# Second operand of the decay scans in two PSUM banks, scans cut to at most three chunk runs, decay copies on ScalarE

## The chip, the core and the metric

The kernel runs on one core of a Trainium2 chip. The metric is the device time of one execution in microseconds (us), smaller is better. The core's engines work side by side, each through its own queue in order: TensorE (PE in the profile; PEld is its weight load), VectorE (DVE), ScalarE (ACT), GpSimd (POOL), and SP, whose queue here issues all transfers (DMA). An engine waits for another through semaphores. SBUF is the working memory of 128 partitions; PSUM is a second, smaller one of eight banks of 512 float32 columns per partition, into which TensorE writes its products.

## What is computed

A recurrent (gated linear) attention over 4 batches, 8 heads, 768 steps and 48 dimensions, then a soft mixture of experts, then a gated MLP with RMS normalisation, on 3,072 tokens of width 384:

```python
for t in range(S):                                   # attention, per batch and head
    state = alpha[t][:, None] * state + outer(k[t], v[t])
    y[t] = q[t] @ state
logits = x @ phi                                     # soft mixture of 8 experts, 32 slots
slot_out = relu(softmax(logits, 0).T @ x @ w1) @ w2  # per expert
x = softmax(logits, 1) @ slot_out
xn = x / rms(x) * rms_g                              # gated MLP
out = (silu(xn @ w_gate) * (xn @ w_val)) @ w_out
```

## The kernel before

**Attention in chunks.** The 768 steps of each batch are cut into chunks of 128, 24 chunks in all. Two heads lie together on the partitions (rows 0 to 47 and 64 to 111), so a chunk has four head pairs. Inside a chunk the decay is taken out of the recurrence: R is the running product of alpha from the chunk's first step, q is multiplied by R, and k by an inverse decay iR, so that the chunk's scores are plain products of k and q, masked to the lower triangle. The state between chunks is multiplied by the chunk's whole decay.

**Preparation of a group.** Chunks are prepared in units of three (the first two units have one and two), each unit in two groups of two head pairs; there are 17 groups. A group is a row of "chunk runs" of 129 columns, one leading column and 128 steps: six runs, 774 columns, in the large groups, four runs, 516 columns, in the first three. For each group:

- `prep_R` (L465, VectorE): one scan over all runs. At each column it multiplies the running value by alpha and takes the maximum with the second operand `d1`, which is 1 at the start of each run (it restarts the product there) and a tiny floor elsewhere.
- `prep_i` (L471, L472, VectorE): reciprocals of the runs' last R are written into `d2`, then one scan backwards over all runs with `d2` as second operand makes iR.
- `prep_c` (L481, L482, GpSimd): two small copies of the runs' whole decay, one for the state (`gm`), one for a check (`chk`).
- `prep_m` (L487, VectorE): k times iR and q times R.

`d1` and `d2` lie in SBUF, in a block of 776 columns each.

**A chunk.** TensorE makes the scores of the head pairs (L523) into two PSUM banks; ScalarE copies these two (L530); GpSimd masks them (L534); TensorE makes the outputs (L559, L566) and the state's update (L546, L550), which VectorE multiplies by the decay (L572, one operand in PSUM, one in SBUF). The scores of even chunks go to the pair of banks `sc`, those of odd chunks to the pair `tr` (`sc_of`, L507).

**Weights beside it.** The gate weights, 64 bits wide in memory, are turned to float32 meanwhile in `wide_ops`: load (L385, SP), L388 and L389 (ScalarE), L392 (VectorE), L399 and L400 (GpSimd), L403 (VectorE); three landing blocks and two sets of temporaries are all they have. The experts' weights (L738 for w1, L740 for w2, 64 loads of 384 KB) go to blocks of SBUF as these come free. The working memory has 58 such blocks.

**What sets the order.** `Plan` is a list scheduler: each step has an engine, a cost, a priority and the ring places it takes (`new`) or uses (`use`). Before any instruction is made, it walks through the steps in time by these costs and fixes the order of each engine's queue, SP's included. The semaphores follow from the data.

After attention, `join`, `experts` (hidden products L751, results L772) and `gated` (72 rounds of L1029, L1031, L1033, L1036 and their products) come in turn.

## Time and profile before

| | |
|---|---|
| three runs | 445.19, 443.86, 442.87 us; median 443.86 |
| profiled execution | 441.4 us; span from first to last instruction 439.7 us |
| busy: TensorE, VectorE, ScalarE, GpSimd | 387.5, 304.6, 222.3, 198.2 us |
| chain that ended last | PE 53%, DVE 17%, POOL 14%, issue 6%, DMA 5%, ACT 2% |
| mean granted clock of TensorE | 0.952 |
| transfers | 65.4 MB, mean 149 GB/s |

The busy times are sums over a span whose parts have different limits, so they don't say what bounds one part; the tables by stretch do. A group is all instructions of one line, engine and form, with their count, busy time, mean duration and the idle time of the engine before them. An instruction that waits for something after it has started shows as a long instruction, not as idle time. The chain is followed back from the last instruction, at each step to what released it.

### The profile page before, as it was taken

How to read it: one execution, taken by the hardware profiler on the slowest of the kernel's cores; microseconds unless marked ns; L12 is line 12 of the kernel's file. 1: busy time of each engine (PE TensorE's matmuls, PEld its weight loads, DVE VectorE, ACT ScalarE, POOL GpSimd, SP SyncE). 2: the span in 40 equal slices, each digit the busy share in tenths (PEclk: the TensorE clock that was granted, in tenths of full speed). 3: DMA queues.
4: the chain of work that ended last, by engine and by line, in shares of the span. 5: the costliest groups of instructions: out<-in, count | busy, mean ns of one | idle time of the engine just before them, and what ended most of it. 6: DMA issues, size and time to landing. Idle time of an engine off the chain costs nothing.

```text
span 439.7 us, 9033 instructions
## 1 busy us (share of the span) xinstructions
PE 387.5 (88%) x3435; PEld 320.4 (73%) x3435; DVE 304.6 (69%) x494; ACT 222.3 (51%) x465; POOL 198.2 (45%) x281
## 2 busy tenths in 40 slices
PE   6688957589488699999987999999999999999994
PEld 6566735466366577764445798999999999999993
DVE  8999798999998978261169987655554655664550
ACT  1424463267345456361277756645546555546441
POOL 3488788869988788141131683130220210310000
PEclk8889996969889869999999999999999999999999
DMA  7879997887575768989932300200101001002002
GB/s 239 270 245 306 288 271 264 256 258 210 149 183 162 233 218 283 337 290 345 382 114 87 108 2 0 73 0 15 59 2 37 35 1 70 3 1 73 1 2 79
DMA packets 28758, 65.43 MB, mean 149 GB/s; under 512 B 4096, under 2 KB 10368, under 8 KB 28704
## 3 DMA queue, kind: packets, MB, share of 16 engines
q1 hardware_dynamic: 28704, 64.75, 45.7%
q8 instruction: 29, 0.48, 0.5%
q14 instruction: 25, 0.20, 0.2%
HBM read 60.01 MB, written 4.72 MB: 147 GB/s over the span
## 4 chain that ended last, share of the span: by engine, by line
PE 53%; DVE 17%; POOL 14%; issue 6%; DMA 5%; ACT 2%; SPq 0%; DVEq 0%; POOLq 0%; ACTq 0%
POOL b L400 4%; POOL b L534 3%; POOL b L399 3%; PE pssc L996 3%; PE pstr L996 3%; DVE b L487 3%; DVE b L465 3%; PE psy L1003 3%; PE pskn L1003 3%; PE psmisc L1005 3%; PE psU L1005 3%; PE pskn L1005 3%; PE psy L1005 3%; PE psU L1003 3%; PE psmisc L1004 3%
## 5 line engine op out<-in xcount | busy, mean ns | idle before, releaser
L1036 DVE TENSOR_TENSOR b<-b,b 128x512 fp32r<-128x512 f32 (+1 forms) x73 | 51.9, 712 | 52.5 <-PE psmisc L1005 24.6
L1033 ACT CAST b<-b 128x512 fp32r<-128x512 f32 (+1 forms) x73 | 44.8, 615 | 46.3 <-DVE b L1031 44.5
L1031 DVE TENSOR_TENSOR b<-b,pssc 128x512 f32<-128x512 f32 (+1 forms) x73 | 49.2, 676 | 15.7 <-ACT b L1029 13.6
L1029 ACT ACTIVATE b<-pstr 128x512 f32<-128x512 f32 (+1 forms) x73 | 43.1, 594 | 31.5 <-PE pstr L996 24.1
L534 POOL TENSOR_SCALAR_AFFINE_SELECT b<-b 128x512 f32<-128x512 f32 x48 | 50.1, 1061 | 13.2 <-ACT b L530 13.1
L559 PE MATMUL psy<-b,b 128*48 128x128 f32 x384 | 32.8, 303 | 11.8 <-POOL b L534 10.3
L388 ACT ACTIVATE b<-b 128x384 f32<-128x384 f32 x36 | 20.2, 562 | 44.9 <-DVE b L403 34.0
L400 POOL TENSOR_TENSOR b<-b,b 128x384 int32<-128x384 int32 x26 | 40.1, 1543 | 2.0
L933 POOL TENSOR_TENSOR sq<-st 128x4 f32<-128x4 f32 x5 | 1.5, 301 | 87.4 <-DVE st L918 87.4
L559 PEld LDWEIGHTS psy<-b,b 128*48 128x48 f32 x384 | 23.9, 135 | 20.7 <-POOL b L534 14.0
L403 DVE SCALAR_TENSOR_TENSOR b<-b,b 128x384 int32<-128x384 int32 x36 | 27.9, 777 | 10.0 <-POOL b L400 10.0
L399 POOL TENSOR_TENSOR b<-b,e 128x384 int32<-128x384 int32 x26 | 29.6, 1139 | 10.8 <-DVE b L392 9.0
L487 DVE TENSOR_TENSOR b<-b,b 128x768 f32<-128x768 f32 (+1 forms) x33 | 34.2, 1066 | 0.3
L465 DVE TENSOR_TENSOR_SCAN b<-b,b 128x774 f32<-128x774 f32 (+1 forms) x17 | 33.9, 1992 | 0.1
L472 DVE TENSOR_TENSOR_SCAN b<-b,b 128x774 f32<-128x774 f32 (+1 forms) x17 | 32.0, 1881 | 0.9
L996 PE MATMUL pssc<-b,b 128*128 128x512 f32 (+1 forms) x73 | 28.7, 394 | 0.4 <-DVE b L1031 0.4
L996 PE MATMUL pstr<-b,b 128*128 128x512 f32 (+1 forms) x73 | 28.6, 392 | 0.1
L1114 ACT COPY y<-psy 128x512 f32<-128x512 f32 x24 | 14.1, 586 | 28.4 <-PE psy L566 23.1
L566 PE MATMUL psy<-b,b 48*48 48x128 f32 x320 | 24.1, 295 | 1.8 <-DVE b L572 1.8
L1005 PE MATMUL pskn<-b,b 128*128 128x384 f32 x72 | 24.5, 341 | 1.1 <-DVE b L1036 1.0
L1003 PE MATMUL pskn<-b,b 128*128 128x384 f32 x72 | 24.8, 345 | 0.0
L1003 PE MATMUL psU<-b,b 128*128 128x384 f32 x72 | 24.5, 340 | 0.0
(241 smaller groups left out, 986.4 us busy)
## 6 DMA issues: line engine op xcount, KB each, us to landing
b<-in_moe_w_dram SPq DMA_DIRECT2D x64, 384.0 KB, 6.1
b<-in_v_rows_dram SPq DMA_DIRECT2D x24, 192.0 KB, 4.4
b<-in_moe_w_gate_dram SPq DMA_DIRECT2D x12, 384.0 KB, 3.8
b<-in_moe_w_out_dram SPq DMA_DIRECT2D x12, 384.0 KB, 5.1
b<-in_moe_w_val_dram SPq DMA_DIRECT2D x12, 384.0 KB, 3.1
out_dram<-b SPq DMA_DIRECT2D x24, 192.0 KB, 1.9
b<-in_alpha_rows_dram SPq DMA_DIRECT2D x24, 145.3 KB, 4.2
b<-in_k_rows_dram SPq DMA_DIRECT2D x18, 144.0 KB, 4.7
```

What stands on the lines that cost most here:

```text
L400: G.tensor_tensor(ui, ui, r(), ALU.add)
L465: V.tensor_tensor_scan(plan("R", (u, g))[:, 0:w], plan("al", (u, g))[:, 0:w], d1[:, 0:w], 1.0, ALU.mult, ALU.max)
L487: eng.tensor_tensor(t, t, r, ALU.mult)
L534: G.affine_select(s, s, pattern=[[0, NP], [1, C]], compare_op=ALU.is_ge, fill=0.0, base=0, channel_multiplier=-1)
L559: T.matmul(y[64 * a:64 * a + D, p, :], vv[:, h], heads(plan("scS", (n, a)))[:, p, :], start=p == 0, stop=first and p == NP - 1)
L996: T.matmul(plan(r, ("gv", j, f))[:, s], G4(f // 3, a)[:, f % 3 * P:(f % 3 + 1) * P], plan("Q", ("c4", j))[:, s].bitcast(F32R), start=True, ...
L1003: T.matmul(po, h, wo_of(f)[:, 0, :], start=(f == 0), stop=False)
L1005: T.matmul(po, l, wo_of(f)[:, 0, :], start=False, stop=(f == NF - 1))
L1029: plan.op(part("sg"), "ACT", 51 + 427 / np, pg, lambda g=g, SG=SG, s=s: A.activation(SG()[:, s], plan(*g)[:, s], AF.Silu), [part("gv"), *p ...
L1031: plan.op(part("mu"), "DVE", 69 + 533 / np, pg, lambda val=val, SG=SG, s=s: V.tensor_tensor(SG()[:, s], SG()[:, s], plan(*val)[:, s], ALU. ...
L1033: plan.op(part("hh"), "ACT", 93 + 427 / np, pg, lambda SG=SG, HH=HH, s=s: A.copy(HH()[:, s], SG()[:, s]), [part("mu"), *pre("hh")], new=ne ...
L1036: lambda SG=SG, HH=HH, HL=HL, s=s: V.tensor_tensor(HL()[:, s], SG()[:, s], HH()[:, s], ALU.subtract), [part("hh"), *pre("hl")], new=new(hl),
```

## The change

The second operands `d1` and `d2` move from two blocks of SBUF to the two PSUM banks `tr`, as wide as three chunk runs and one column. Scans and reciprocals therefore go over at most three runs at a time: two pieces for each group (of three runs, 387 columns, or of two, 258). The `tr` banks are taken from the start by a step without an engine (`pb`) and come free when the last inverse scan is planned (`pe`); until then, and also after, the scores of all chunks use the `sc` banks alone. The two small copies of a group go from GpSimd to ScalarE, with a cost of 400 ns in place of 450. The two blocks of SBUF are free for weights from the start. Nothing else is edited; since the planner sees other places and costs, the order of the steps in attention changes too. Lines of the changed kernel are 3 to 12 higher than before.

```diff
--- before.py
+++ after.py
@@ -281,10 +281,10 @@
 
     BL, CW = 768, 384
     LAY = [("wT", BL, 2 * KD * FF // BL), ("Tk", BL, PLACES["k"]), ("Tq", BL, PLACES["q"]), ("al", BCOLS, PLACES["a"]), ("R", BCOLS, 3), ("iR", BCOLS, 2), ("scS", NP * C, 4), ("St", NP * D, 2),
-           ("knS", DM, 1), ("vt", DM, 5), ("cv", 2 * CW, 3), ("cu", CW, 2), ("cr", CW, 2), ("d1", BCOLS, 1), ("d2", BCOLS, 1),
+           ("knS", DM, 1), ("vt", DM, 5), ("cv", 2 * CW, 3), ("cu", CW, 2), ("cr", CW, 2),
            ("fa", 2 * NP * NCH, 1), ("mask", C, 1), ("chk", NP * NCH, 1), ("gm", NP * J, 3)]
 
-    GROUPS = [set(s.split()) for s in ("wT", "Tk", "Tq", "al", "R", "iR", "scS St fa mask chk gm", "knS vt", "cv", "cu cr", "d1", "d2")]
+    GROUPS = [set(s.split()) for s in ("wT", "Tk", "Tq", "al", "R", "iR", "scS St fa mask chk gm", "knS vt", "cv", "cu cr")]
     room, inside, where = [], [], {}
     for nm, size, n in LAY:
         for i in range(n):
@@ -348,11 +348,14 @@
         return t.rearrange("k (n p) -> k n p", n=NP)
 
     St = [heads(t) for t in rings["St"]]
-    d1, d2, mask, chk = (rings[x][0] for x in ("d1", "d2", "mask", "chk"))
+    mask, chk = (rings[x][0] for x in ("mask", "chk"))
+
+    RUNS = 3
+    d1, d2 = (banks["tr"][i][:, 0:RUNS * (C + 1) + 1] for i in range(2))
     chk = chk.rearrange("p (a b) -> p a b", a=NP)
     phiP = rings["phi"][0].rearrange("p (n s) -> p n s", n=NP)
     V.memset(d1, FLOOR)
-    V.memset(d1[:, 0:6 * C1].rearrange("p (m x) -> p m x", x=C1)[:, :, 0:1], 1.0)
+    V.memset(d1[:, 0:RUNS * C1].rearrange("p (m x) -> p m x", x=C1)[:, :, 0:1], 1.0)
     V.memset(d2, FLOOR)
     V.memset(banks["y"][0], 0.0)
     V.memset(banks["U"][0][:, 0:NP * D], 0.0)
@@ -459,17 +462,25 @@
 
         return t[:, at:at + units[u][2][g][1] * units[u][1] * C1].rearrange("k (m x) -> k m x", x=C1)
 
+    def scans(u, g):
+        m = units[u][1] * units[u][2][g][1]
+        n = -(-m // RUNS)
+        return [(m * i // n * C1, m * (i + 1) // n * C1) for i in range(n)]
+
     def prep_R(u, g):
 
-        w = PIECES["a"][u, g][0] - 1
-        V.tensor_tensor_scan(plan("R", (u, g))[:, 0:w], plan("al", (u, g))[:, 0:w], d1[:, 0:w], 1.0, ALU.mult, ALU.max)
+        al, R = plan("al", (u, g)), plan("R", (u, g))
+        for x, y in scans(u, g):
+            V.tensor_tensor_scan(R[:, x:y], al[:, x:y], d1[:, 0:y - x], 1.0, ALU.mult, ALU.max)
 
     def prep_i(u, g):
 
-        w = slice(1, PIECES["a"][u, g][0])
-        al = plan("al", (u, g))
-        V.reciprocal(runs(d2, u, g, 1)[:, :, C:C1], runs(plan("R", (u, g)), u, g)[:, :, C:C1])
-        V.tensor_tensor_scan(plan("iR", (u, g))[:, w][:, ::-1], al[:, w][:, ::-1], d2[:, w][:, ::-1], 1.0, ALU.mult, ALU.max)
+        al, R, iR = plan("al", (u, g)), plan("R", (u, g)), plan("iR", (u, g))
+        for x, y in scans(u, g):
+            run = lambda t: t.rearrange("k (m x) -> k m x", x=C1)[:, :, C:C1]
+            w, d = slice(x + 1, y + 1), d2[:, 1:y - x + 1]
+            V.reciprocal(run(d), run(R[:, x:y]))
+            V.tensor_tensor_scan(iR[:, w][:, ::-1], al[:, w][:, ::-1], d[:, ::-1], 1.0, ALU.mult, ALU.max)
 
     def prep_c(u, g):
 
@@ -478,8 +489,8 @@
         pc = lambda t: t.rearrange("k (p c) x -> k p c x", c=j)
         if g == 0:
             gmU[u] = plan("gm", u).rearrange("k (p c) -> k p c", c=J)
-        G.tensor_copy(gmU[u][:, p0:p0 + n, 0:j], pc(runs(plan("R", (u, g)), u, g))[:, :, :, C])
-        G.tensor_copy(chk[:, p0:p0 + n, c0:c0 + j], pc(runs(plan("iR", (u, g)), u, g))[:, :, :, 1])
+        A.copy(gmU[u][:, p0:p0 + n, 0:j], pc(runs(plan("R", (u, g)), u, g))[:, :, :, C])
+        A.copy(chk[:, p0:p0 + n, c0:c0 + j], pc(runs(plan("iR", (u, g)), u, g))[:, :, :, 1])
 
     def prep_m(nm, u, g, eng):
         t = plan(RING[nm], (u, g))[:, 0:PIECES[nm][u, g][0]].rearrange("k (m x) -> k m x", x=C)
@@ -504,7 +515,7 @@
         return [(r, (u, g)) for g in range(len(units[u][2]))]
 
     def sc_of(n):
-        return [("tr" if n % 2 else "sc", (n, a)) for a in range(2)]
+        return [("sc", (n, a)) for a in range(2)]
 
     def turn_k(n, p):
         T.transpose(heads(plan("kn", n))[:, p, :], kq("Tk", n, p), ident)
@@ -1062,6 +1073,7 @@
         plan.op(("wu", i), "PE", 436, 1e6, lambda i=i: warm(plan("misc", ("wu", i)), 4), new=[("misc", ("wu", i))])
 
 
+    plan.op("pb", "X", 0, 0, lambda: None, new=[("tr", "d1"), ("tr", "d2")])
     plan.op("phi", "SP", 900, 0, load_phi, [("v", 1)])
     last = {}
     for u, (c0, j, groups) in enumerate(units):
@@ -1073,7 +1085,7 @@
                 last[nm] = [("l", nm, x)]
             plan.op(("R", x), "DVE", 40 + 2.3 * w, t, lambda x=x: prep_R(*x), [("l", "a", x)], new=[("R", x)], use=[("al", x)])
             plan.op(("I", x), "DVE", 220 + 2.3 * w, t, lambda x=x: prep_i(*x), [("R", x)], new=[("iR", x)], use=[("R", x), ("al", x)])
-            plan.op(("ck", x), "Pool", 450, t + CK, lambda x=x: prep_c(*x), [("I", x), *([("ck", (u, 0))] if g else [])], new=[] if g else [("gm", u)], use=[("R", x), ("iR", x)])
+            plan.op(("ck", x), "ACT", 400, t + CK, lambda x=x: prep_c(*x), [("I", x), *([("ck", (u, 0))] if g else [])], new=[] if g else [("gm", u)], use=[("R", x), ("iR", x)])
             for nm in "kq":
                 e, en, cost = (G, "Pool", 2.6 * w) if (nm, u) in BY_POOL else (V, "DVE", 60 + 1.05 * w)
                 plan.op((nm, x), en, cost, t, lambda nm=nm, x=x, e=e: prep_m(nm, *x, e), [("l", nm, x), ("R" if nm == "q" else "I", x)],
@@ -1115,7 +1127,7 @@
         plan.op(("x", n), "PE", 436, n + XD, lambda n=n: xnat(n), [("ye", n)], new=[x_bank(n)], use=[("yT", n)])
         plan.op(("xe", n), "ACT", 480, n + XD, lambda n=n: move_x(n), [("x", n)], new=[("xN", n)], use=[x_bank(n)])
 
-    plan.op("pe", "X", 0, 0, lambda: None, [x for x in plan.ops if x[0] == "I"], new=[("d1", 0), ("d2", 0)])
+    plan.op("pe", "X", 0, 0, lambda: None, [x for x in plan.ops if x[0] == "I"], use=[("tr", "d1"), ("tr", "d2")])
     plan.op("se", "X", 0, 0, lambda: None, [("o", NCH - 1)], new=[("St", 0), ("St", 1), ("mask", 0)])
     for i in range(NCH // 4):
         group(plan, i, phiP, NP, 4 * i + 3 + GD)
```

VectorE's queue, the preparation of one group in mid attention. Before; `b_142` is `d1`, `b_143` is `d2`, L392 and L403 belong to the gate weights:

```order
L465 SCALAR_TENSOR_TENSOR b_125<-b_124,b_142 128x774
L392 TENSOR_SCALAR b_140<-b_140 128x384
L403 SCALAR_TENSOR_TENSOR b_103<-b_137,b_140 128x384
L471 RECIPROCAL b_143<-b_125 128x6
L472 SCALAR_TENSOR_TENSOR b_129<-b_124,b_143 128x774
L403 SCALAR_TENSOR_TENSOR b_103<-b_138,b_140 128x384
L487 TENSOR_TENSOR b_117<-b_117,b_129 128x768
L487 TENSOR_TENSOR b_122<-b_122,b_125 128x768
```

After; `pstr_63` is `d1`, `pstr_64` is `d2`:

```order
L474 SCALAR_TENSOR_TENSOR b_125<-b_124,pstr_63 128x387 x2
L406 SCALAR_TENSOR_TENSOR b_103<-b_137,b_140 128x384
L395 TENSOR_SCALAR b_140<-b_140 128x384
L482 RECIPROCAL pstr_64<-b_125 128x3
L483 SCALAR_TENSOR_TENSOR b_129<-b_124,pstr_64 128x387
L482 RECIPROCAL pstr_64<-b_125 128x3
L483 SCALAR_TENSOR_TENSOR b_129<-b_124,pstr_64 128x387
L498 TENSOR_TENSOR b_117<-b_117,b_129 128x768
```

Each scan and the reciprocal have become two (`x2` is the pair in one row), with 387 columns in place of 774, and a reciprocal stands ahead of each backward piece.

ScalarE's queue, a little earlier in the program, around the copies of one chunk's scores. Before; the L388 and L389 are the gate weights' first steps:

```order
L582 COPY x<-psmisc_70 128x384
L388 ACTIVATE b_140<-b_138 128x384
L389 ACTIVATE b_141<-b_138 128x384
L530 COPY b_132<-pstr_63 128x512
L530 COPY b_133<-pstr_64 128x512
L388 ACTIVATE b_140<-b_139 128x384
L389 ACTIVATE b_141<-b_139 128x384
L1114 COPY y_146<-psy_69 128x512
L388 ACTIVATE b_140<-b_137 128x384
```

After (L391 and L392 are the gate weights, L541 the score copies, L492 and L493 the decay copies):

```order
L593 COPY x<-psmisc_70 128x384
L391 ACTIVATE b_140<-b_139 128x384
L392 ACTIVATE b_141<-b_139 128x384
L541 COPY b_130<-pssc_65 128x512
L541 COPY b_131<-pssc_66 128x512
L492 COPY b_130<-b_127 128x6
L493 COPY b_133<-b_128 128x2x3
L391 ACTIVATE b_140<-b_137 128x384
L392 ACTIVATE b_141<-b_137 128x384
L528 COPY b_134<-pskn_67 128x384
```

The scores come from `pssc` alone, and the two decay copies of a group stand in this queue, here behind the score copies and ahead of the next gate weight.

SP's queue at about a third of the preparation. Before (L738 are expert weights):

```order
L385 DMA b_138<-in_moe_w_gate_dram 128x768
L453 DMA b_118<-in_q_rows_dram 48x768 x2
L738 DMA b_879<-in_moe_w_dram 128x768
L456 DMA b_135<-in_v_rows_dram 128x384 x2
L453 DMA b_124<-in_alpha_rows_dram 48x775 x2
L385 DMA b_139<-in_moe_w_gate_dram 128x768
L453 DMA b_114<-in_k_rows_dram 48x768 x2
L453 DMA b_119<-in_q_rows_dram 48x768 x2
```

After (L749 are expert weights):

```order
L388 DMA b_138<-in_moe_w_gate_dram 128x768
L456 DMA b_118<-in_q_rows_dram 48x768 x2
L749 DMA b_949<-in_moe_w_dram 128x768
L459 DMA b_135<-in_v_rows_dram 128x384
L749 DMA b_959<-in_moe_w_dram 128x768
L749 DMA b_962<-in_moe_w_dram 128x768
L388 DMA b_139<-in_moe_w_gate_dram 128x768
L459 DMA b_135<-in_v_rows_dram 128x384
L388 DMA b_137<-in_moe_w_gate_dram 128x768
```

Three expert loads stand where one stood.

## Rows read from the trace of the kernel before

**Rows 1.** Stretches: busy us of each engine, granted clock, DMA share, GB/s.

```profile
0.00:168.00 168.00, 129.24 (x1581) 98.05 (x1581) 152.95 (x202) 78.53 (x174) 133.20 (x136) 0.88 0.78 238
168.00:194.00 26.00, 25.18 (x367) 19.26 (x367) 13.79 (x44) 13.42 (x34) 12.92 (x22) 1.00 0.94 324
194.00:222.00 28.00, 26.46 (x344) 12.23 (x344) 5.30 (x17) 6.69 (x16) 4.62 (x15) 1.00 0.92 340
```

**Rows 2.** Chain of waits, 20 to 168 us: shares by line.

```profile
by line: issue 13.4%; POOL b L400 11.4%; POOL b L534 10.3%; POOL b L399 10.1%; DVE b L487 5.7%; DVE b L403 4.7%; DMA b<-in_moe_w_gate_dram 4.7%; DVE b L472 4.1%; DVE b L465 4.1%; PE psy L559 3.1%; DVE b L392 3.0%; POOL b L482 2.5%; PE pssc 
```

**Rows 3.** Groups on VectorE, 0 to 168 us: count, busy us, mean ns, idle.

```profile
L465 DVE TENSOR_TENSOR_SCAN b<-b,b 128x774 f32<-128x774 f32 x14 | 30.2, 2157 | 0.0
L487 DVE TENSOR_TENSOR b<-b,b 128x768 f32<-128x768 f32 x28 | 30.0, 1100 | 0.2
L472 DVE TENSOR_TENSOR_SCAN b<-b,b 128x774 f32<-128x774 f32 x14 | 28.3, 2020 | 0.8
L403 DVE SCALAR_TENSOR_TENSOR b<-b,b 128x384 int32<-128x384 int32 x24 | 19.8, 824 | 9.0 <-POOL b L400 9.0
...
L472 DVE TENSOR_TENSOR_SCAN b<-b,b 128x516 f32<-128x516 f32 x3 | 3.7, 1232 | 0.2
...
L471 DVE RECIPROCAL b<-b 128x6 f32<-128x6 f32 x14 | 2.6, 184 | 0.1
```

**Rows 4.** Groups on GpSimd, 0 to 168 us.

```profile
L534 POOL TENSOR_SCALAR_AFFINE_SELECT b<-b 128x512 f32<-128x512 f32 x42 | 46.1, 1114 | 8.2 <-ACT b L530 8.1
L400 POOL TENSOR_TENSOR b<-b,b 128x384 int32<-128x384 int32 x24 | 37.9, 1578 | 1.9
L399 POOL TENSOR_TENSOR b<-b,e 128x384 int32<-128x384 int32 x24 | 27.9, 1162 | 10.5 <-DVE b L392 8.7 <-ACT b L388 1.7
L482 POOL COPY b<-b 128x6 f32<-128x6 f32 (+1 forms) x17 | 11.9, 702 | 7.4 <-DVE b L472 3.5 <-PE pstr L523 1.9 <-PE psmisc L629 1.9
L481 POOL COPY b<-b 128x6 f32<-128x6 f32 (+1 forms) x17 | 10.2, 598 | 1.7 <-DVE b L465 1.6
```

**Rows 5.** Order of time, 71.3 to 73 us: start us, us, instruction.

```profile
71.45 0.35 DVE L572 TENSOR_TENSOR b<-psU,b 128x192 f32<-128x192 f32 x1
71.61 0.83 POOL L399 TENSOR_TENSOR b<-b,e 128x384 int32<-128x384 int32 x1 [0.95 <-DVE b L392]
...
71.71 2.35 DVE L465 TENSOR_TENSOR_SCAN b<-b,b 128x774 f32<-128x774 f32 x1
...
72.52 2.33 POOL L400 TENSOR_TENSOR b<-b,b 128x384 int32<-128x384 int32 x1
```

**Rows 6.** Order of time on VectorE around 51 us.

```profile
51.01 1.77 DVE L472 TENSOR_TENSOR_SCAN b<-b,b 128x774 f32<-128x774 f32 x1
```

**Rows 7.** Single lines: shortest, median and longest instruction in ns.

```profile
L572 DVE TENSOR_TENSOR b<-psU,b x20: 325/344/358, 23.5 to 183.5; 128x192 f32<-128x192 f32 x20
...
L399 POOL TENSOR_TENSOR b<-b,e x26: 824/856/2291, 36.5 to 170.6; 128x384 int32<-128x384 int32 x26
...
L400 POOL TENSOR_TENSOR b<-b,b x26: 992/1198/2349, 37.4 to 171.6; 128x384 int32<-128x384 int32 x26
...
L534 POOL TENSOR_SCALAR_AFFINE_SELECT b<-b x48: 630/760/2147, 11.7 to 181.2; 128x512 f32<-128x512 f32 x48
```

**Rows 8.** Single lines: second operand in PSUM (L1031), in SBUF (L487).

```profile
L1031 DVE TENSOR_TENSOR b<-b,pssc x73: 415/686/691, 237.1 to 427.4; 128x512 f32<-128x512 f32 x71, 128x256 f32<-128x256 f32 x2
...
L487 DVE TENSOR_TENSOR b<-b,b x33: 683/951/1637, 6.3 to 167.0; 128x768 f32<-128x768 f32 x28, 128x512 f32<-128x512 f32 x5
```

**Rows 9.** Waits of ScalarE, 0 to 168 us: us, times, longest.

```profile
ACT b L388 <- DVE b L403: 34.0, 13, 5.9
```

**Rows 10.** Order of time on TensorE, 213 to 223 us.

```profile
221.41 1.48 PE L772 MATMUL pskn<-b,x 128*32 128x384 f32 x10 [1.54 <-DMA b<-in_moe_w_dram]
```

**Rows 11.** Groups on ScalarE, whole span: score copies, smallest instruction.

```profile
L530 ACT COPY b<-pssc 128x512 f32<-128x512 f32 x24 | 13.3, 602 | 3.8 <-PE pssc L523 3.8
...
L704 ACT ACTIVATE sm<-sm 128x1 f32<-128x1 f32 x1 | 0.2, 203 | 0.1
```

## The prediction

> **What bounds the kernel now.** I read the table of stretches first [rows 1]. The kernel has three parts: attention up to about 194 us, the experts to 222 us, the gated MLP after that. In the planner's order of instructions, everything from the last chunks of attention on is the same before and after (on TensorE the last 2,686 of 3,262 rows). So the change can only act on attention's first 168 us, in which the scans run, and on the weight loads that run beside them. [...]
>
> The chain of waits says who holds whom [rows 2]. GpSimd's three costly lines (L400, L534, L399) make up 32% of the chain from 20 to 168 us; the two scans, L465 and L472, only 8%. That is more than GpSimd's work should cost, and the next views say why. In the order of time [rows 5], the VectorE instruction L572, whose one operand is in PSUM, takes 0.35 us, and GpSimd's L399 runs through beside it in 0.83 us, its floor [rows 7]. Then scan L465, with both operands in SBUF, starts at 71.71 while L399 is still running and takes 2.35 us; an undisturbed scan of this size takes 1.77 us [rows 6]. L400 starts inside the scan, takes 2.33 us where its floor is 0.99 [rows 7], and ends 0.8 us after the scan does. Each has waited for the other: the scan until L399 was through, L400 until the scan was. All 20 of L572 lie between 325 and 358 ns [rows 7], although 17 of them overlap a GpSimd instruction. The trace thus says that a VectorE instruction with an operand in PSUM and one in SBUF is outside this exclusion. That is what the change makes of 34 scans.
>
> **The change, part by part.** Negative is saved; all counts are for the first 168 us.
>
> *The scans' own waiting.* L465 has 14 large ones at 2.157 us, L472 14 at 2.020 [rows 3], against 1.77: 14 x 0.387 + 14 x 0.250 = 8.9 us, which should go: -8.9.
>
> *Cutting them in two.* From 774 to 516 columns a scan goes from 1.77 to 1.23 us [rows 3, 6]: 2.09 ns a column, so 0.15 us of it is fixed. Each of the 17 groups gets one more scan in each direction: 34 x 0.15 = 5.1 us. Each gets one more reciprocal of 0.184 us: 17 x 0.184 = 3.1 us. Together +8.2 on VectorE, nothing hides it. The reciprocals now write to PSUM, which no row shows: I keep 0.184 us; at L572's 0.35, far wider and with PSUM, all 34 would cost 5.6 more. No scan here reads PSUM, so its price there is bounded. Two-operand instructions of 512 columns take 686 ns (median, mostly that size) with an operand in PSUM and 683 at best with both in SBUF [rows 8]. I take no difference; as upper bound a scan that still pays all its present waiting, +8.9. [...]
>
> *GpSimd's waiting.* Against the floors [rows 4, 7], L400 loses 24 x (1.578 - 0.992) = 14.1 us, L399 24 x (1.162 - 0.824) = 8.1, L534 42 x (1.114 - 0.630) = 20.3: 42.5 us. L400 and L399 mostly stand behind scans, L534 also behind other two-operand instructions, so 22 to 42 us go with the scans; I take 30. The 34 small copies, 11.9 + 10.2 = 22.1 us [rows 4], leave GpSimd altogether. So 133 us become about 81, and GpSimd stops being second in the chain. This saves nothing by itself; it does through the next two.
>
> *VectorE's waits for GpSimd.* L403 stands idle 9.0 us for L400 [rows 3]. With GpSimd at half load I take -6, between 0 and -9.
>
> *Exclusion on VectorE's other instructions.* From L1031's 415 and 686 ns at 256 and 512 columns [rows 8], a column costs 1.06 ns, so L487 (768 columns) should take 0.955 and L403 (384) about 0.55 us. They take 1.100 and 0.824 [rows 3]: 28 x 0.145 + 24 x 0.274 = 10.6 us lost. GpSimd can now work through 66 us of scans (30.2 + 28.3 and six small ones) undisturbed, nearly all of its 81, so fewer meetings are left. I take half, -5.3, between 0 and -10.6.
>
> *The copies on ScalarE.* 34 x 0.2 us (its smallest instruction [rows 11]) = 7 us, at most 34 x 0.6 = 20 (a score copy's price, for 85 times the columns), on an engine that is busy 78.5 of 168 us [rows 1]: cost nothing, covered by its idle time. But they wait for the group's last scan, and what stands behind them waits too (a rival below).
>
> *One pair of banks for the scores.* The next chunk's scores can start only when ScalarE has made both copies, 2 x 0.60 us [rows 11]. In the order, the score sets that stood back to back are now apart, with the previous chunk's other products between them, and those products wait for GpSimd's masks on the same scores anyway. I take +2; bounds 0 and 24 chunks x 1.2 = 29.
>
> *Two more blocks for weights.* SP's order has three expert loads where it had one before the queue's next alpha pieces, so two loads come earlier. They take 2 x 384 KB, at 340 GB/s [rows 1] 2.3 us. They matter at the end: TensorE waits for the last expert load at 221.41, 1.54 us of it before that instruction [rows 10]. Transfers fill 0.78 x 168 + 0.94 x 26 + 0.92 x 28 = 181 of 222 us, so they fit into 12 us less. What frees their blocks is the end of the preparation and the experts' products, which move along, and the two early loads keep the last one from becoming the new wait. I set it at 0.
>
> Sum: -8.9 + 8.2 - 6 - 5.3 + 2 = **-10 us**. The profiled execution took 441.4 us (span 439.7), so it would take 431.4. It lies 2.5 us below the median of the three runs, 443.86. The prediction is for the median: **434 us**.
>
> **The rivals.** *Slower, by ScalarE's queue.* ScalarE already stands 34.0 us for L403, 13 times [rows 9]; now 17 more waits come, each for an inverse scan. In its new order 4 of the 17 pairs stand right in front of a score copy. A late scan then holds the copies, the copies hold the only score banks, TensorE stands, and its masks and outputs with it. The gain of 12 is used up once each of 24 chunks loses 0.5 us. At 0.7 us it is 443.9 - 12 + 17 = 449. For it: waits in that queue are common and up to 5.9 us long. Against it: the weights' preparation, which makes those waits, gets faster by GpSimd's relief.
>
> *The exclusion stays* (scans hold GpSimd out wherever the operand is), so that the change does not do what it says. Then the cut costs 8.2, the copies' 22 us off GpSimd return perhaps 6 of it through L403's waits: 446. Against it: L572 [rows 5, 7].
>
> *Half of it is lost to TensorE or transfers.* VectorE finishes 12 us earlier, but TensorE, with 129 us of work in the 168, has more left to do after, or a load comes late: -5, 439. For it: DMA shares of 0.92 to 0.94 in the stretches after [rows 1].
>
> *More than that.* All bounds come in: -0.7 - 9 - 10.6 = -20, with 2 for the banks -18: 426. For it: the chain's 32% of GpSimd is 47 us of 148.
>
> **How the numbers follow.** Forecast 0.50 (430 to 438), more 0.13, half 0.20, exclusion stays 0.06, ScalarE's queue 0.11. The range is 425 to 444: it leaves out the far end of "more", about 0.05, and most of the two cases above 444, about 0.15. A difference under 0.5% (2.2 us) can't be told from none here. Faster by more, under 441.6: 0.49 + 0.13 + 0.16 = 0.78. Slower by more: 0.09 of the queue and 0.02 of the other, 0.11. The rest, 0.11, is no change.
>
> **What would show it.** Right: two scans of 387 columns at about 0.95 us each, whatever GpSimd does; L399 and L400 near 0.83 and 1.0 us beside them; GpSimd's busy time in attention down by some 50 us; the last scan's end about 12 us earlier, and the gated MLP as long as before. Wrong: scans well above 1 us, or ones beside which L400 still takes over 2 us (the exclusion stays); score matmuls waiting for L530's copies and those for the decay copies (ScalarE's queue); attention ending earlier with a longer wait for expert weights behind it (half).

## The result and the profile after

The changed kernel takes 432.01 us (median of four executions, 430.92 to 432.55), the kernel before 444.08 us (four, 442.87 to 445.19); the ratio is 0.973, with a 95% interval of 0.970 to 0.976. The forecast was 434 us in 425 to 444. The profiled execution after took 430.92 us (span 429.2); the spans differ by 10.5 us.

In the lists below, lines stand 3 to 12 higher than in the rows of before: L474 and L483 are the scans, L482 the reciprocal, L498 the products, L402, L403 and L406 the gate weights' last steps, L545 the masks. First the stretches: length, busy us of PE, PEld, DVE, ACT and POOL with counts, granted clock, DMA share, GB/s.

```profile
0.00:154.00 154.00, 126.37 (x1569) 96.83 (x1570) 142.46 (x254) 81.41 (x205) 81.44 (x103) 0.84 0.89 263
154.00:184.00 30.00, 28.51 (x385) 21.87 (x385) 12.77 (x45) 14.70 (x37) 11.92 (x21) 0.94 0.79 281
184.00:210.50 26.50, 26.16 (x340) 11.65 (x339) 4.96 (x16) 7.09 (x17) 4.63 (x15) 1.00 0.89 331
210.50:222.00 11.50, 9.27 (x80) 5.17 (x80) 10.00 (x29) 9.05 (x24) 4.00 (x4) 1.00 0.40 135
222.00:226.00 4.00, 3.90 (x16) 2.51 (x16) 3.45 (x9) 2.93 (x7) 2.01 (x2) 0.63 0.01 2
226.00:230.00 4.00, 4.00 (x14) 3.24 (x14) 3.95 (x10) 3.76 (x11) 0.00 (x0) 0.50 0.01 2
230.00:234.00 4.00, 4.00 (x15) 3.61 (x14) 2.35 (x5) 1.53 (x4) 2.01 (x2) 0.59 0.31 98
234.00:429.20 195.20, 187.62 (x1027) 179.12 (x1025) 113.15 (x184) 106.42 (x199) 39.76 (x101) 1.00 0.09 30
```

Against [rows 1]: the first row now ends 14 us earlier, with GpSimd busy 81.44 us where it was 133.20, and DMA at 0.89 where it was 0.78. The second row, the rest of attention and the join, has a clock of 0.94 where it was 1.00. In the three rows from 222 to 234 TensorE's granted clock is 0.50 to 0.63, behind a stretch in which it was busy 9.27 of 11.5 us.

VectorE's groups of the same 154 us (count, busy us, mean ns, idle us before them), to be held against [rows 3]:

```profile
L498 DVE TENSOR_TENSOR b<-b,b 128x768 f32<-128x768 f32 x28 | 29.6, 1076 | 0.2
L483 DVE TENSOR_TENSOR_SCAN b<-b,pstr 128x387 f32<-128x387 f32 x28 | 26.9, 959 | 1.2
L474 DVE TENSOR_TENSOR_SCAN b<-b,pstr 128x387 f32<-128x387 f32 x28 | 25.1, 938 | 0.0
L406 DVE SCALAR_TENSOR_TENSOR b<-b,b 128x384 int32<-128x384 int32 x24 | 16.9, 703 | 0.0
...
L482 DVE RECIPROCAL pstr<-b 128x3 f32<-128x3 f32 x28 | 5.0, 178 | 0.5
```

GpSimd's, against [rows 4]:

```profile
L545 POOL TENSOR_SCALAR_AFFINE_SELECT b<-b 128x512 f32<-128x512 f32 x42 | 32.1, 783 | 33.1 <-ACT b L541 32.9
L403 POOL TENSOR_TENSOR b<-b,b 128x384 int32<-128x384 int32 x24 | 25.9, 1079 | 1.9
L402 POOL TENSOR_TENSOR b<-b,e 128x384 int32<-128x384 int32 x25 | 22.5, 899 | 33.1 <-DVE b L395 17.5 <-ACT b L541 4.1 <-ACT b L392 4.0
```

A scan of 387 columns takes 0.94 or 0.96 us on average. L406 stands idle 0.0 us where L403 stood 9.0. The masks went from 1,114 to 783 ns, L400 from 1,578 to 1,079, L399 from 1,162 to 899; the small copies are gone from GpSimd.

Order of time, VectorE and GpSimd, in one group's backward scans (start us, us, instruction):

```profile
95.76 0.83 POOL L402 TENSOR_TENSOR b<-b,e 128x384 int32<-128x384 int32 x1 [1.37 <-DVE b L395]
...
95.81 0.96 DVE L483 TENSOR_TENSOR_SCAN b<-b,pstr 128x387 f32<-128x387 f32 x1
96.67 1.01 POOL L403 TENSOR_TENSOR b<-b,b 128x384 int32<-128x384 int32 x1
...
97.02 0.96 DVE L483 TENSOR_TENSOR_SCAN b<-b,pstr 128x387 f32<-128x387 f32 x1
...
97.63 0.63 POOL L545 TENSOR_SCALAR_AFFINE_SELECT b<-b 128x512 f32<-128x512 f32 x1
```

The answer to [rows 5]: scan and GpSimd run side by side. L402 and L403 take 0.83 and 1.01 us, next to their floors of [rows 7], and neither scan waits: each takes 0.96 us.

The chain of waits, 20 to 154 us, shares by line:

```profile
by line: DMA b<-in_k_rows_dram 10.0%; DVE b L483 8.7%; DMA b<-in_q_rows_dram 8.5%; DMA b<-in_moe_w_val_dram 8.3%; DVE b L498 8.0%; DVE b L474 6.5%; PE psy L570 5.6%; DVE b L406 5.4%; PE psy L577 5.3%; issue 4.9%; PE pssc L534 3.1%; DMA b<-i
```

GpSimd had 32% of it in [rows 2]. Now no GpSimd line is among the leading ones, and transfers have the first, third and fourth place.

**Where the 10.5 us of span lie.** The preparation (last L487 or L498) ends at 153.6 us instead of 167.9: -14.3. From there to the start of the last output products of attention (L577, before L566) it takes 20.8 us instead of 17.3: +3.5. The expert products (L751 to L772) take 26.5 instead of 28.1: -1.6. The gated MLP behind them takes 218.7 instead of 216.8: +1.9.

Of the kernels in the table below, four had disturbed executions (two of four with the fourth landing block alone, the profiled one among them; one of six with the transposes, with the planner's cost, and with later loads and transposes together); their medians and ratios leave these out, and the profile of the fourth block alone is not read.

### The profile page after: what moved, and what is told of

Its sections match the earlier page's. It is cut to its first block, busy times and chain, and to the rows that moved or that the text cites. A ratio compares the mean times of both kernels' runs of the same rounds, so it can differ in the third digit from the quotient of the medians.

```text
span 429.2 us, 9081 instructions
## 1 busy us (share of the span) xinstructions
PE 389.8 (91%) x3435; PEld 324.0 (75%) x3435; DVE 293.1 (68%) x545; ACT 226.9 (53%) x499; POOL 145.8 (34%) x247
## 4 chain that ended last, share of the span: by engine, by line
PE 58%; DVE 19%; DMA 14%; issue 4%; POOL 2%; ACT 1%; SPq 1%; DVEq 0%; ACTq 0%; POOLq 0%
DVE b L483 4%; DMA b<-in_moe_w_val_dram 4%; PE pssc L1007 4%; PE pstr L1007 4%; DVE b L474 3%; DMA b<-in_k_rows_dram 3%; DVE b L498 3%; PE pskn L1014 3%; PE pskn L1016 3%; PE psU L1014 3%; PE psmisc L1014 3%; PE psU L1016 3%; PE psy L1016 3%; PE psmisc L1016 3%; PE pskn L1015 3%
## 5 line engine op out<-in xcount | busy, mean ns | idle before, releaser
L545 POOL TENSOR_SCALAR_AFFINE_SELECT b<-b 128x512 f32<-128x512 f32 x48 | 35.8, 765 | 39.7 <-ACT b L541 39.5
L534 PE MATMUL pssc<-b,b 48*128 48x128 f32 x384 | 34.2, 311 | 3.9 <-ACT b L541 1.6
L391 ACT ACTIVATE b<-b 128x384 f32<-128x384 f32 x36 | 20.4, 568 | 29.1 <-DMA b<-in_moe_w_gate_dram 10.6
L402 POOL TENSOR_TENSOR b<-b,e 128x384 int32<-128x384 int32 x26 | 23.3, 896 | 36.1 <-DVE b L395 20.5
L534 PEld LDWEIGHTS pssc<-b,b 48*128 48x128 f32 x384 | 28.2, 208 | 8.7 <-ACT b L541 3.1
L498 DVE TENSOR_TENSOR b<-b,b 128x768 f32<-128x768 f32 (+1 forms) x33 | 33.0, 1020 | 0.3
L541 ACT COPY b<-pssc 128x512 f32<-128x512 f32 x48 | 26.5, 590 | 10.6 <-PE pssc L534 10.6
L483 DVE TENSOR_TENSOR_SCAN b<-b,pstr 128x387 f32<-128x387 f32 (+1 forms) x34 | 31.0, 912 | 1.4
L590 PE MATMUL psmisc<-ident,y 128*128 128x128 f32 x92 | 17.3, 317 | 13.9 <-ACT x L593 7.5
L474 DVE TENSOR_TENSOR_SCAN b<-b,pstr 128x387 f32<-128x387 f32 (+1 forms) x34 | 29.0, 892 | 0.9 <-DMA b<-in_alpha_rows_dram 0.9
L403 POOL TENSOR_TENSOR b<-b,b 128x384 int32<-128x384 int32 x26 | 27.9, 1072 | 2.0
L406 DVE SCALAR_TENSOR_TENSOR b<-b,b 128x384 int32<-128x384 int32 x36 | 25.3, 704 | 2.8 <-POOL b L403 2.8
L395 DVE TENSOR_SCALAR b<-b 128x384 f32<-128x384 f32 x36 | 18.1, 502 | 11.0 <-ACT b L391 10.9
```

The source lines that it names most:

```text
L474: V.tensor_tensor_scan(R[:, x:y], al[:, x:y], d1[:, 0:y - x], 1.0, ALU.mult, ALU.max)
L483: V.tensor_tensor_scan(iR[:, w][:, ::-1], al[:, w][:, ::-1], d[:, ::-1], 1.0, ALU.mult, ALU.max)
L498: eng.tensor_tensor(t, t, r, ALU.mult)
L534: T.matmul(heads(plan(*sc_of(n)[a]))[:, p, :], kq("Tk", n, p)[r], kq("Tq", n, p)[r], start=True, stop=True)
```

## The experiments

All fourteen kernels in one table. "Preparation" is the end of the last L487 or its successor, "tail" the time from there to the start of the last output products, both from the profile; scans is the sum of all scans' durations (count times mean). Ratios are to the kernel before, run on the same chip beside each.

| kernel | median us | ratio, 95% interval | preparation | tail | scans |
|---|---|---|---|---|---|
| before | 444.08 | 1 | 167.9 | 17.3 | 65.9 |
| after | 432.01 | 0.973 (0.970 to 0.976) | 153.6 | 20.8 | 61.3 |
| after, two blocks reserved | 434.09 | 0.981 (0.977 to 0.986) | 152.2 | 22.3 | 61.3 |
| the same, operands in these blocks | 456.94 | 1.033 (1.028 to 1.037) | 170.9 | 27.4 | 81.1 |
| after, copies on GpSimd | 431.12 | 0.974 (0.969 to 0.978) | 154.4 | 18.5 | 61.3 |
| before, copies on ScalarE | 451.36 | 1.020 (1.015 to 1.026) | 168.1 | 27.3 | 64.8 |
| before, scans cut | 446.13 | 1.006 (1.002 to 1.009) | 170.6 | 17.3 | 82.0 |
| before, one pair for scores | 444.11 | 1.001 (0.997 to 1.005) | 170.0 | 17.3 | 65.7 |
| copies on GpSimd + transposes | 430.08 | 0.968 (0.964 to 0.972) | 155.8 | 18.1 | 61.4 |
| copies on GpSimd + planner's cost | 430.82 | 0.971 (0.967 to 0.975) | 155.4 | 18.2 | 61.4 |
| copies on GpSimd + later expert loads | 427.78 | 0.964 (0.958 to 0.969) | 153.2 | 17.3 | 61.3 |
| copies on GpSimd + fourth landing block | 427.75 | 0.963 (0.956 to 0.971) | - | - | - |
| fourth block + transposes | 430.48 | 0.968 (0.964 to 0.973) | 159.1 | 17.3 | 61.4 |
| later expert loads + transposes | 424.75 | 0.957 (0.952 to 0.961) | 152.6 | 18.8 | 61.4 |

### Is it the place of the operand?

Two kernels whose instructions start in the same order on every engine, but for the first two scans, some 4 us into the span, which change places with a few start-up instructions. The first is the changed kernel with the two blocks of SBUF reserved as before:

```diff
-           ... ("cu", CW, 2), ("cr", CW, 2),
+           ... ("cu", CW, 2), ("cr", CW, 2), ("d1", BCOLS, 1), ("d2", BCOLS, 1),
-    plan.op("pe", ..., use=[("tr", "d1"), ("tr", "d2")])
+    plan.op("pe", ..., new=[("d1", 0), ("d2", 0)], use=[("tr", "d1"), ("tr", "d2")])
```

> The changed kernel, but two blocks of working memory stay reserved until the last inverse scan, as before the change; the scans' second operands stay in PSUM. Theory (the exclusion between the scans and GpSimd is the cause): the two early blocks are worth at most the two loads' 2.3 us, so 432 to 434.5 us, and GpSimd's busy time stays near 146 us. Rival (freed blocks let the weights come earlier): 437 us or more, with a longer wait for the last expert load near the end of the experts.

The second puts the operands into these blocks and changes nothing else:

```diff
-    d1, d2 = (banks["tr"][i][:, 0:RUNS * (C + 1) + 1] for i in range(2))
+    d1, d2 = (rings[x][0][:, 0:RUNS * (C + 1) + 1] for x in ("d1", "d2"))
```

> The kernel with the two blocks reserved, and the scans' second operands put into these two blocks of SBUF; everything else, the order of every queue included, is the same as in that kernel (cut scans, copies on ScalarE, scores on one pair of banks). Theory (exclusion): scans of 387 columns go from a steady 0.93 to 0.96 us to a mean of 1.1 us or more, GpSimd's three lines rise by some 25 to 30 us again, and the time is 8 to 14 us above that kernel, 442 to 447 us. Rival (the new order, the copies' move and the cut make the gain, wherever the operand lies): within 3 us of that kernel.

Measured: 434.09 against 456.94 us. The place alone is worth 22.8 us, against the 8 to 14 expected: 18.7 of it lie in the preparation's end, with 19.8 us of scan durations behind that, and 5.1 in the tail, which the expectation did not name; the rest is about 1 us shorter. The same piece of program as in the timeline above, now with both operands in SBUF:

```profile
103.83 0.83 POOL L402 TENSOR_TENSOR b<-b,e 128x384 int32<-128x384 int32 x1 [3.00 <-DVE b L482]
103.88 1.61 DVE L483 TENSOR_TENSOR_SCAN b<-b,b 128x387 f32<-128x387 f32 x1
...
104.74 1.54 POOL L403 TENSOR_TENSOR b<-b,b 128x384 int32<-128x384 int32 x1
...
105.73 1.38 DVE L483 TENSOR_TENSOR_SCAN b<-b,b 128x387 f32<-128x387 f32 x1
...
106.24 1.29 POOL L545 TENSOR_SCALAR_AFFINE_SELECT b<-b 128x512 f32<-128x512 f32 x1
```

L402 comes first and takes its 0.83 us; the scan beside it takes 1.61 where it took 0.96. L403 starts inside the scan and takes 1.54 where it took 1.01; the next scan takes 1.38 for 0.96 and the mask L545 beside it 1.29 for 0.63. This is the exclusion that [rows 5] showed, switched on by the place of one operand.

An undisturbed scan of 258 columns costs the same from either place, to 2 ns. L474's shortest, median and longest in ns, first with the operand in PSUM (the changed kernel), then in SBUF:

```profile
L474 DVE TENSOR_TENSOR_SCAN b<-b,pstr x34: 666/933/954, 3.5 to 146.9; 128x387 f32<-128x387 f32 x28, 128x258 f32<-128x258 f32 x6
```

```profile
L474 DVE TENSOR_TENSOR_SCAN b<-b,b x34: 668/1323/1758, 3.7 to 162.2; 128x387 f32<-128x387 f32 x28, 128x258 f32<-128x258 f32 x6
```

The shortest (258 columns) are 666 and 668 ns.

Reserving the two blocks cost 2.1 us by the medians and 3.9 by the ratios, 0.981 (0.977 to 0.986) against 0.973 (0.970 to 0.976), whose intervals just fail to meet: the blocks for weights are worth a little. By the theory the two early loads were worth at most 2.3 us.

### The copies, with and without the rest

```diff
-        A.copy(gmU[u][...], ...)
-        A.copy(chk[...], ...)
+        G.tensor_copy(gmU[u][...], ...)
+        G.tensor_copy(chk[...], ...)
-            plan.op(("ck", x), "ACT", 400, ...)
+            plan.op(("ck", x), "Pool", 450, ...)
```

> The changed kernel with the two decay copies back on GpSimd at their old cost. Theory (exclusion): most of the gain stays. Without scans in their way the copies cost GpSimd about 34 x 0.3 = 10 us of the 70 that it has idle in the preparation, so 432 to 437 us. Rival (the move of the copies is what helps): 439 us or more.

Measured: 431.12 us, just under the theory's 432 to 437. Once the operands are in PSUM, moving the copies is worth nothing that can be told. The reverse edit on the kernel before, copies to ScalarE and nothing else:

> The kernel before with the two decay copies moved to ScalarE at the new cost, and nothing else: scans whole, operands in SBUF, scores on two pairs of banks. Theory (exclusion): GpSimd loses 22 us of busy time but still waits behind scans, so a gain of 0 to 4 us, 440 to 444 us. Rival (the move of the copies is what helps): 436 us or less.

Measured: 451.36 us, 2.0% slower; theory and rival both miss. The preparation ends where it did (168.1), the tail takes 27.3 us instead of 17.3. TensorE around the tail's start (columns as above):

```profile
160.00:164.00 4.00, 1.20 (x24) 0.61 (x20) 3.97 (x5) 1.55 (x5) 3.92 (x4) 1.00 0.91 329
164.00:168.00 4.00, 2.29 (x10) 1.57 (x10) 3.68 (x5) 0.71 (x3) 1.95 (x2) 0.50 0.59 202
168.00:172.00 4.00, 4.00 (x33) 3.40 (x34) 3.61 (x8) 1.52 (x3) 3.19 (x4) 0.50 0.89 270
...
176.00:180.00 4.00, 1.68 (x34) 1.23 (x27) 1.06 (x3) 1.35 (x3) 0.65 (x1) 1.00 0.56 215
...
184.00:188.00 4.00, 4.00 (x36) 2.89 (x36) 1.54 (x5) 2.13 (x5) 1.27 (x2) 0.50 0.63 241
```

It is busy for 3.49 of the 8 us from 160 to 168, its clock falls to 0.50, rises to 1.00 again, and falls to 0.50 a second time behind 176 to 180, where it is busy for 1.68 of 4 us. What TensorE waited for from 160 to 184 us (us, times, longest):

```profile
PE psmisc L579 <- DVE acc L640: 3.9, 1, 3.9
PE pskn L510 <- ACT b L517: 2.3, 1, 2.3
```

L640 stands in VectorE's queue behind a gate weight and a backward scan of 2.17 us; L517 is a copy on ScalarE that stood in its queue behind a gate weight's first step, which waited for its transfer (6.17 us on the chain). So the price of the copies is paid in the tail, partly with TensorE's clock at 0.50. The table has it in every kernel: with the copies on ScalarE the tail takes 20.8 to 27.4 us, with the copies on GpSimd 17.3 to 18.8. That the moved copies shift the planner's order there, rather than hold ScalarE themselves, is argued from these waits and was not tried.

### The cut alone

The kernel before with the scans of at most three runs, operands in SBUF: `scans`, `prep_R` and `prep_i` as in the change, and

```diff
-    d1, d2, mask, chk = (rings[x][0] for x in ("d1", "d2", "mask", "chk"))
+    mask, chk = (rings[x][0] for x in ("mask", "chk"))
+    RUNS = 3
+    d1, d2 = (rings[x][0][:, 0:RUNS * (C + 1) + 1] for x in ("d1", "d2"))
```

> The kernel before with its scans and reciprocals cut into two pieces of at most three runs, and nothing else: operands in SBUF, copies on GpSimd, scores on two pairs of banks. Theory (exclusion; cutting by itself only costs): VectorE gets 8 us more of fixed cost and still waits for GpSimd, so the preparation ends 3 to 10 us later than at 168 us, 446 to 454 us. Rival (shorter scans hold GpSimd out for less long, so cutting is itself a gain): 441 us or less.

Measured: 446.13 us, 0.6% slower, the low end. VectorE's groups, 0 to 171 us:

```profile
L474 DVE TENSOR_TENSOR_SCAN b<-b,b 128x387 f32<-128x387 f32 x28 | 39.4, 1445 | 0.0
L483 DVE TENSOR_TENSOR_SCAN b<-b,b 128x387 f32<-128x387 f32 x28 | 33.3, 1190 | 1.2
...
L406 DVE SCALAR_TENSOR_TENSOR b<-b,b 128x384 int32<-128x384 int32 x24 | 17.8, 742 | 0.9 <-POOL b L403 0.9
```

Two pieces meet GpSimd twice: a forward piece takes 1,445 ns on average, half a microsecond over the 938 of the changed kernel. All scans together take 16.1 us more than before, yet the preparation ends only 2.6 us later. Of the rest 8.1 us came back in L406's idle time (9.0 before, 0.9 here): what a scan waits for GpSimd, the next gate weight need not. And count times mean holds some time twice, since the second piece of a forward scan starts a little before the first ends: by busy time the scans take 80.7 us against 65.9, 14.8 more. The cut costs 2.4 us in the kernel's time, against the kernel before beside it; alone it brings nothing.

### One pair of banks alone

```diff
-        return [("tr" if n % 2 else "sc", (n, a)) for a in range(2)]
+        return [("sc", (n, a)) for a in range(2)]
```

> The kernel before with the scores of all chunks on one pair of banks, and nothing else. Theory: the pair is worth little, the next scores find the copies done, 0 to 4 us: 443 to 448 us. Rival (TensorE stands for ScalarE's copies in each of 24 chunks): 454 us or more.

Measured: 444.11 us, no difference. The second pair of banks was not needed.

### TensorE's clock, and the planner's cost

On the kernel with copies on GpSimd, 16 transposes of the identity, whose result is not used, behind the last product with the gate weights (`gates`):

```diff
+            if (r, kk) == (1, KD - 1):
+                warm(banks["misc"][0], 16)
```

> The changed kernel with the copies on GpSimd, and 16 more transposes of the identity on TensorE behind the last gate product, where TensorE stands idle for some 2 us at 220 us; their result is not used. Theory (the 2 us that the gated MLP takes longer than before are the granted clock of 0.5 that follows this idle time): the clock there stays at 1.00 and the time falls by 1 to 3 us against the 431.1 of the kernel without them, 428 to 430 us. Rival (the MLP is longer for another reason): 430.5 us or more, and the same length from 209 us to the end.

Measured: 430.08 us, the upper end of the theory's bracket. Without them TensorE is busy 2.20 of the 4 us from 216 and its clock is 0.50, 0.50 and 0.72 in the next three stretches of 4 us:

```profile
216.00:220.00 4.00, 2.20 (x27) 0.75 (x20) 3.69 (x12) 2.22 (x6) 1.22 (x2) 1.00 0.61 170
220.00:224.00 4.00, 3.87 (x15) 2.37 (x16) 2.68 (x7) 1.54 (x3) 1.00 (x1) 0.50 0.08 31
```

With them:

```profile
216.00:220.00 4.00, 4.00 (x46) 1.65 (x49) 3.76 (x11) 3.68 (x12) 1.97 (x2) 1.00 0.02 6
220.00:224.00 4.00, 4.00 (x34) 2.83 (x28) 3.69 (x14) 1.91 (x5) 0.67 (x2) 1.00 0.63 197
224.00:228.00 4.00, 3.57 (x16) 1.95 (x15) 3.72 (x10) 3.22 (x8) 1.37 (x2) 1.00 0.00 0
228.00:232.00 4.00, 4.00 (x22) 3.74 (x22) 3.92 (x9) 4.00 (x12) 0.91 (x1) 1.00 0.14 38
```

The clock stays at 1.00, but in this profile the last expert weight came 1.6 us late, and the gain of 1.0 us is not told apart from none by the intervals. Nor does the clock fall in every execution without transposes. In the profile of before TensorE is busy for no more, and the clock holds:

```profile
230.00:234.00 4.00, 2.10 (x23) 0.83 (x16) 3.65 (x13) 1.94 (x5) 0.91 (x1) 1.00 0.74 243
234.00:238.00 4.00, 3.56 (x19) 1.95 (x17) 3.72 (x10) 2.83 (x8) 1.66 (x2) 1.00 0.11 45
```

On the base with copies on GpSimd, 400 ns more for a backward scan in the planner, for the pieces it does not know of:

```diff
-            plan.op(("I", x), "DVE", 220 + 2.3 * w, t, ...)
+            plan.op(("I", x), "DVE", 620 + 2.3 * w, t, ...)
```

> The changed kernel with the copies on GpSimd, and the planner's cost of an inverse scan raised by 400 ns to what its two pieces and second reciprocal take. Theory (the order was made for another cost, which leaves a few us of waits): 426 to 430.5 us. Rival (transfers bound the preparation now, so that the order matters little): 430.5 to 432.5 us.

Measured: 430.82 us, in the rival's range; the planner's wrong cost costs nothing here that can be told.

### What bounds it next

A fourth landing block for the 64-bit weights, in one of the two freed blocks:

```diff
-           ("knS", DM, 1), ("vt", DM, 5), ("cv", 2 * CW, 3), ...
+           ("knS", DM, 1), ("vt", DM, 5), ("cv", 2 * CW, 4), ...
```

> Against the kernel with only the operands moved to PSUM (431.12 us; its preparation ends at 154.4 us). There ScalarE stands 12.5 us between 100 and 215 us for loads of 64-bit weights, and the chain of the last 45 us of attention has its largest share in one such load (11.4%). Theory, transfers are the next bound and the three landing blocks are what makes them late: with a fourth landing block, taken from the two blocks that the change freed, these waits fall under 5 us, the preparation ends 1 to 4 us earlier, time 426 to 429.5. Rival, the transfers as a whole are the bound (share 0.89 of the 16 DMA engines in the preparation) and it does not matter which block they land in: the waits move to other loads, preparation's end within 1 us, 430 to 432.5.

> The fourth landing block together with the 16 transposes (their result is not used) that keep TensorE busy at the start of the gated MLP. If the two are independent: about 1 us under the kernel with the fourth block alone, so 425 to 428.5 by the theory; by the rival (transfers as a whole) about the time with the transposes alone, 430.1, give or take 1.

Alone, the median of 427.75 us lies in the theory's bracket, but it rests on two executions, 425.93 and 429.57 us, too far apart to settle it. With the transposes it took 430.48, the same as the transposes without it, as the rival had it, and the preparation ended at 159.1 us, 3.3 later. ScalarE's waits for these loads between 100 and 215 us had fallen all the same: from 10.2 us on the base, for the `in_moe_w_val` loads alone, to at most 3.6, the shortest of its nine leading waits, none of which is for such a load. The chain from 20 to 154 us now held an alpha load of 7.63 us. There the theory of the landing blocks fails: the waits fell, and the preparation did not end earlier.

The expert loads, four chunks later in the planner's priority:

```diff
-            plan.op(("w", *x), "SP", 1092, 4 + i * 0.3, ...)
+            plan.op(("w", *x), "SP", 1092, 8 + i * 0.3, ...)
```

> Same base, but the planner gives the expert weights' loads a priority four chunks later (8 in place of 4), so fewer of them run beside the preparation. Theory, transfers are the next bound in the preparation: ScalarE's 12.5 us of waits for loads of 64-bit weights fall, the preparation ends 1 to 3 us earlier, and TensorE waits a little longer for expert weights at their end, time 428 to 432. Rival, the loads' order does not bind the preparation but the experts need every early load: preparation's end unchanged, expert products end 2 us or more later, 433 to 437.

Measured: 427.78 us, under the theory's bracket. ScalarE's waits for loads of 64-bit weights, 100 to 215 us (us, times, longest), on the base and with the later loads:

```profile
ACT b L391 <- DMA b<-in_moe_w_val_dram: 10.2, 6, 2.8
...
ACT b L391 <- DMA b<-in_moe_w_out_dram: 2.3, 1, 2.3
```

```profile
ACT b L391 <- DMA b<-in_moe_w_val_dram: 3.8, 4, 2.1
...
ACT b L391 <- DMA b<-in_moe_w_out_dram: 2.0, 1, 2.0
```

They fall from 12.5 to 5.8 us, the preparation ends 1.3 us earlier, the tail is 1.2 shorter, and TensorE still waits only 0.3 us for the last expert weight. So the order of the transfers seems to bind on this base; whether it does so by these waits, the next kernel tests too. Last, both together:

> The later expert loads together with the 16 transposes (their result is not used) at the start of the gated MLP. The later loads alone took 427.78 us; there the granted clock was 0.72, 0.50 and 0.75 in the 15 us from 215 on, where TensorE was busy for only 3.09 of 5 us before it. If the transposes keep the clock at 1.00 there and the two edits are independent: 425 to 427.5 us. Rival, the transposes' own 2 us stand on TensorE's path and take back what the clock gives: 427.5 to 429 us.

Measured: 424.75 us, a little under the theory's bracket; ratio 0.957 (0.952 to 0.961). Behind the transposes:

```profile
215.00:219.00 4.00, 4.00 (x34) 2.56 (x27) 3.66 (x14) 1.57 (x5) 0.49 (x2) 1.00 0.62 201
219.00:223.00 4.00, 3.57 (x17) 2.01 (x16) 3.72 (x10) 3.13 (x8) 1.93 (x2) 1.00 0.00 0
```

Without the transposes these two stretches had 0.78 and 0.50. This is the fastest version of the study, 7.3 us under the changed kernel; that the transposes alone bring the last 3.0 is not secured, since the intervals of the last two kernels overlap.

The later loads help on both bases, without the transposes (0.974 to 0.964) and with them (0.968 to 0.957). But the waits named above do not explain it. The same waits of ScalarE, 100 to 215 us, in this last kernel:

```profile
ACT b L391 <- DMA b<-in_moe_w_val_dram: 12.9, 6, 4.3
ACT b L391 <- DMA b<-in_moe_w_out_dram: 2.2, 1, 2.2
```

They are 15.1 us, more than the 12.5 of the base, and still its preparation ends at 152.6 us, 1.8 earlier than the base's. In the changed kernel with two blocks reserved they are 15.2 us, with the earliest end of all, 152.2. What the later loads relieve stays open.

## Why the prediction was right

**The mechanism** was the one forecast. The operand's place decides whether a scan and GpSimd exclude each other: +22.8 us when it alone is put back. The other parts cost, alone, 0.6% (the cut), 2.0% (the copies) and nothing (one pair), and 3.3% together when the operands lie in SBUF; the operand's place pays for them and makes the whole gain. The rival "the exclusion stays" is out. So is ScalarE's queue as a loss of the size that the rival gave it: the medians with the copies on ScalarE and on GpSimd lie 0.9 us apart.

**The terms**, in us:

| term | predicted | measured |
|---|---|---|
| scans: waiting gone, cut in two | -8.9 + 5.1 | -4.6 (65.9 to 61.3) |
| reciprocals (17 at 184 ns, now 34 at 178) | +3.1 | +2.9 |
| VectorE idle for GpSimd's L400 | -6 | -9.0 (9.0 to 0.0) |
| L487 and L403 shorter | -5.3 | -3.6 (28 x 0.024 + 24 x 0.121) |
| copies on ScalarE | 0 | 0.9 by the medians, not told from 0 (tail +2.3, preparation -0.8) |
| one pair of banks | +2 | 0 (one pair alone) |
| blocks for weights | 0 | -2 to -4 (blocks reserved) |
| GpSimd busy in the preparation | about 81 | 81.4 |

The first four make -14.3, and the preparation ends 14.3 us earlier, where the prediction's own four made -12. The agreement is closer than the method, and in part luck: in the kernel with the cut alone the same four (+16.1, +2.7, -8.1 and -1.6, with L403's successor at 742 and the products at 1,113 ns) make +9, and its preparation ends 2.6 us later, so some 6 us of the 9 did not reach its end.

**What the prediction put at zero or wrong.** It let the change act on the first 168 us alone, with the MLP as long as before. The tail grew by 3.5 us: a transfer of 5.7 us (the 64-bit `in_moe_w_val`), which ScalarE waits for, stands at the head of its chain, and TensorE's clock is 0.94 there. This transfer starts at 154.3 us, behind an expert load; with the copies on GpSimd the transfer at the head of that chain starts at 149.5, and the tail takes 18.5 us. So about 2.3 of the 3.5 us go with the moved copies, the term put at 0; that SP's order is the way is argued from these chains. It is the rival "half of it is lost to TensorE or transfers", in part: it took a quarter of the gain. The MLP grew by 1.9 us, with a clock of 0.50 to 0.63 from 222 to 234 us. A clock under 1.00 there is not tied to the change: the kernels with the cut alone and with one pair, whose order is close to that of before, have it too (mean 0.97 and 0.98 behind 228 us, where the profile of before has 1.00). The profiled execution of before had a mean clock of 0.952; of 48 others beside later runs, 47 had 0.915 to 0.942 and one 0.955. The sum stood on a favourable execution, 2.7 us under its kernel's median, where the profiled one after lies 1.1 us under its own. So the medians are 12.1 us apart and the spans 10.5.

The misses nearly cancel, which is luck, so the sum of -10 became -10.5: -3.0 (L403's waits), -2 (banks), -1.6 (experts), -0.8 (scans) and -0.2 (reciprocals) against +3.5 (tail), +1.9 (MLP) and +1.7 (L487 and L403).

**The cover of the copies.** The prediction costed them at nothing because ScalarE has idle time. In the changed kernel that holds for the time, though not for the tail (ScalarE 81.41 us busy of 154, and 6.9 us of waits for scans ahead of the copies). On the kernel before it does not: +7.3 us by the medians, with TensorE's clock at 0.50 in part of the tail. An idle engine did not make the step free. That the order of the queues around it decided is argued from the waits above; no run holds that order fixed and moves the copies alone.

## What to carry to other kernels

Where VectorE and GpSimd are both busy, look in the order of time for pairs in which each is long by the other's length, and move one of VectorE's two operands to PSUM where a bank is to be had, even at the price of cutting the instruction: here the place was worth 22.8 us, and the cut alone cost 2.4. Once that wait is gone, read the chain again before polishing the rest: here transfers had taken its place, and a later priority for loads that were not yet needed brought 3.3 us by the medians, the moved copies nothing that can be told. Of a change in several parts, run each part alone: here the place of the operand was worth all of the gain, and the moved copies, alone, cost 2%.

## What the runs showed that was not expected

Cutting a scan while both operands are in SBUF makes all scans together 16 us longer (65.9 to 82.0), and the kernel only 2.4 us slower. Small copies of 0.2 us each, moved to an engine that is half idle (busy 82.35 of 168.1 us with them), made the kernel 2% slower, with TensorE waiting and then at a clock of 0.50: busy 1.20 of 4 us, then 8 us at that clock. With 2 us of transposes without a use that clock was 1.00 in the 12 us after them, where it had been 0.50 to 0.72; the profile of before held 1.00 without them. And ScalarE's waits for transfers, which looked like the next bound, were longer in the fastest kernel of the study (15.1 us between 100 and 215 us) than in its base (12.5).
